# A SwiGLU feed-forward kernel on one core: three pairs of junk matmuls become two whole-array ones, and one early projection group also waits for x rows 768-1023

## The chip, the core and the metric

The kernel runs on one core of one Trainium2 chip. The core has a matmul engine (PE, with its weight loads shown apart as PEld), three elementwise engines (DVE, ACT, POOL), an engine that issues most transfers (SP) and 16 DMA engines that carry them. The metric is the device time of one launch in microseconds; the median of three runs before the change is 115.67 us (115.45 to 115.80). Lower is better.

## What is computed

```python
B, S, D, F = 1, 2048, 512, 1376        # all inputs bf16
def reference(x, w_gate, w_up, w_down):
    g = _silu(x @ w_gate)
    u = x @ w_up
    return (g * u) @ w_down
```

x is 2048 x 512, w_gate and w_up are 512 x 1376, w_down is 1376 x 512, the output is 2048 x 512.

## The kernel before, in words

Tokens are cut into four chunks c = 0 to 3 of 512; the 1376 hidden columns into ten F tiles ft = 0 to 9 of 128 and a rest of 96. x is needed with D on the partitions: the first 256 tokens are loaded plainly and transposed on PE with an identity, all later ones come in through transposing DMAs (L279). F tiles 0 to 3 of chunk 0 and 0 to 2 of chunk 1 are computed in the plain way ("classic"): a gate group and an up group of matmuls into one PSUM bank each, silu on ACT, and the product of the two on DVE into `h_sb`. Each group is eight matmuls (L424): four steps over D, each in two halves of 64 output rows that run side by side in the array.

All other F tiles are computed in 2 x 2 blocks (two F tiles by two chunks) with seven block products in place of eight (a Strassen-Winograd scheme). That needs sums of weight blocks (`ss_sb`, made by POOL, with casts by ACT) and sums of x blocks (`tt_sb`). For the first pair of chunks the four x sums T1 to T4 are made by DVE (L337, 128x1024 elements each) and the remaining operand is cast by ACT (L541); POOL's further weight sums stand behind T4. The products run on PE as L616 (fp32 sums) and L628 (plain bf16). The down projection follows (L726, L754, L864, L876).

Every piece of work is entered into a plan. PE's and SP's orders are the order of entry; ACT, DVE and POOL take, at each step of a simulated clock, whichever piece can start first, so the modelled landing times of loads (`land`) move pieces on these engines. From the finished order the plan derives semaphore waits; a wait that an earlier one on the same engine already implies is dropped. A PE instruction that needs several semaphores is preceded by a wait instruction of its own.

The loads that matter here, in SP's order: `xn` (tokens 0-255), `wg0` and `x0b` (gate columns 0-255, tokens 256-511), `wu0` (up columns 0-255), `wg2`, `wu2` (columns 256-511), `x1a` (tokens 512-767), `x1b` (tokens 768-1023), `wg4`, `wu4`, `wg8`, `wu8` and so on. Their semaphores are named below by number: s_dma14 xn, s_dma30 wg0, s_dma22 x0b, s_dma21 wu0, s_dma29 wg2, s_dma20 wu2, s_dma0 x1a, s_dma1 x1b, s_dma12 wg4, s_dma28 wu4, s_dma2 wg8, s_dma3 wu8.

While the first loads are under way PE runs matmuls on constant ones, into banks nobody reads (L350, L353 and, between the transposes and the first projection, L397). The program order of PE is then: chunk 0 gate tiles 0 and 1, up tiles 0 and 1, gate tiles 2 and 3, up tiles 2 and 3, then chunk 1.

## Time and profile before

| what | value |
|---|---|
| median of three runs | 115.67 us (115.45 to 115.80) |
| the profiled execution's own time | 115.52 us |
| its span, first to last instruction | 114.2 us |
| ACT busy, DVE busy, POOL busy | 64.0, 76.5, 62.2 us |
| bytes read from and written to HBM | 4.75 MB and 2.10 MB |

The profile shows one execution. Each engine has its instructions with start and duration; "idle before" is the time in which the engine had nothing running, with what ended it. The chain of waits is the path that ended last, followed back from the last instruction. For a DMA the profile gives the issue and the time from issue to landing, that is until the last part of its semaphore arrived. The difference between the span and the execution's own time, 1.3 us, lies outside the instructions and is taken as fixed.

### The profile page before, as it was taken

Reading aid. Unit: us, or ns where it says so; the run is one execution under the profiler, and the core shown is the slowest. Engines: PE = TensorE matmul, PEld = TensorE weight load, DVE = VectorE, ACT = ScalarE, POOL = GpSimd, SP = SyncE. Lnnn points to the kernel's source line nnn. Section 1 sums busy time; section 2 is a strip of 40 time slices with the busy share of each in tenths; the row PEclk is TensorE's granted clock in tenths of the full one; section 3 lists DMA queues with packets and bytes.
Section 4 is the critical chain, followed back from the end, with each engine's and each line's share of the span. In section 5 each row is a group of like instructions: output and inputs, shape, how many; then the busy total and the mean of one; then the engine's idle time right before and its main releaser. Section 6 shows DMA issues by size and latency. Waiting matters only on the chain.

```text
span 114.2 us, 1765 instructions
## 1 busy us (share of the span) xinstructions
PE 110.7 (97%) x646; PEld 68.0 (60%) x654; DVE 76.5 (67%) x113; ACT 64.0 (56%) x123; POOL 62.2 (54%) x61
## 2 busy tenths in 40 slices
PE   7999999999999999999999999999999999999993
PEld 2665555456674858576776858653344557866452
DVE  0113799883956858493948668499999957486423
ACT  5344765866679895867678786740567960000000
POOL 1493004999999999999998999845000000000000
PEclk9999999999999999999999999999999999999999
DMA  3999999994000000000000000000031002227976
GB/s 101 235 276 237 321 190 225 271 361 101 0 0 0 3 0 3 0 0 6 0 3 0 0 0 0 0 0 0 17 127 46 0 0 46 46 52 183 201 200 197
DMA packets 22808, 9.84 MB, mean 86 GB/s; under 512 B 12848, under 2 KB 22672, under 8 KB 22800
## 3 DMA queue, kind: packets, MB, share of 16 engines
q1 hardware_dynamic: 20656, 8.69, 31.5%
q10 hardware_dynamic: 2144, 1.05, 3.2%
q8 instruction: 5, 0.08, 0.3%
q14 instruction: 3, 0.02, 0.1%
HBM read 4.75 MB, written 2.10 MB: 60 GB/s over the span
## 4 chain that ended last, share of the span: by engine, by line
PE 96%; DVE 1%; issue 1%
PE psum L616 32%; PE psum L726 15%; PE psum L628 12%; PE psum L424 11%; PE psum L864 10%; PE psum L876 4%; PE psum L488 3%; PE psum L754 3%; PE psum L350 2%; PE psum L435 2%; PE psum L514 2%; DVE o_sb L326 1%; PE psum L397 0%; PE psum L380 0%; PE psum L373 0%
## 5 line engine op out<-in xcount | busy, mean ns | idle before, releaser
L616 PE MATMUL psum<-tt_sb,ss_sb 128*128 128x512 f32 x160 | 40.0, 403 | 0.0
L616 PEld LDWEIGHTS psum<-tt_sb,ss_sb 128*128 128x128 f32 x160 | 29.7, 188 | 7.9 <-DVE ts_sb L337 0.6
L337 DVE TENSOR_TENSOR ts_sb<-r_sb,psum 128x512 f32<-128x512 f32 x32 | 20.6, 681 | 14.9 <-ACT r_sb L325 14.9
L337 POOL TENSOR_TENSOR h_sb<-sg_sb,ts_sb 128x512 bf16<-128x512 f32 x16 | 20.9, 1309 | 2.8 <-ACT sg_sb L332 2.8
L332 ACT ACTIVATE sg_sb<-psum 128x512 f32<-128x512 f32 x24 | 14.3, 599 | 11.2 <-PE psum L616 6.0
L325 ACT ACTIVATE r_sb<-psum 128x512 f32<-128x512 f32 x32 | 17.3, 594 | 4.5 <-PE psum L616 4.5
L337 DVE TENSOR_TENSOR h_sb<-sg_sb,psum 128x512 bf16<-128x512 f32 x24 | 16.3, 681 | 4.2 <-PE psum L424 3.9
L337 POOL TENSOR_TENSOR ss_sb<-w_sb 128x512 fp32r<-128x512 bf16 (+1 forms) x12 | 11.8, 997 | 12.6 <-DVE tt_sb L337 9.0
L726 PE MATMUL psum<-wd_sb,h_sb 128*128 128x512 bf16 (+2 forms) x98 | 17.9, 336 | 0.2 <-issue 0.2
L628 PE MATMUL psum<-xT_sb,w_sb 128*128 128x512 bf16 x59 | 14.2, 380 | 0.4 <-issue 0.2
L726 PEld LDWEIGHTS psum<-wd_sb,h_sb 128*128 128x128 bf16 x100 | 8.3, 98 | 9.2 <-issue 1.0
L424 PE MATMUL psum<-xT_sb,w_sb 128*64 128x512 bf16 (+1 forms) x128 | 12.8, 359 | 0.0
L332 ACT ACTIVATE sg_sb<-ts_sb 128x512 f32<-128x512 f32 x16 | 10.1, 634 | 1.6 <-DVE ts_sb L337 1.6
L424 PEld LDWEIGHTS psum<-xT_sb,w_sb 128*64 128x64 bf16 x128 | 7.3, 114 | 5.4 <-DMA w_sb<-in_w_up_dram 0.3
L628 PEld LDWEIGHTS psum<-xT_sb,w_sb 128*128 128x128 bf16 x64 | 5.5, 98 | 8.0 <-issue 2.5
L326 DVE COPY psum<-psum 128x512 f32<-128x512 f32 x8 | 5.6, 699 | 1.2 <-PE psum L616 0.5
L337 POOL TENSOR_TENSOR ss_sb<-w_sb,ss_sb 128x512 fp32r<-128x512 bf16 (+1 forms) x6 | 6.0, 1007 | 0.3
L337 POOL TENSOR_TENSOR ss_sb<-ss_sb,w_sb 128x512 fp32r<-128x512 f32 (+1 forms) x6 | 6.0, 1000 | 0.0
L326 DVE CAST o_sb<-psum 128x512 bf16<-128x512 f32 (+2 forms) x6 | 3.0, 512 | 4.2 <-PE psum L726 3.1
L337 POOL TENSOR_TENSOR ss_sb<-wd_sb 128x640 fp32r<-128x640 bf16 x4 | 5.6, 1406 | 0.0
L864 PE MATMUL psum<-tt_sb,ss_sb 128*128 128x512 f32 x20 | 5.6, 417 | 0.0
L864 PE MATMUL psum<-th_sb,ss_sb 128*128 128x512 f32 x20 | 5.5, 411 | 0.0
(72 smaller groups left out, 121.4 us busy)
## 6 DMA issues: line engine op xcount, KB each, us to landing
wd_sb<-in_w_down_dram SPq DMA_DIRECT2D x1, 1280.0 KB, 8.5
w_sb<-in_w_gate_dram SPq DMA_DIRECT2D x4, 256.0 KB, 4.0
w_sb<-in_w_up_dram SPq DMA_DIRECT2D x4, 256.0 KB, 4.2
out_dram<-o_sb SPq DMA_DIRECT2D x7, 128.0 KB, 1.8
out_dram<-xT_sb ACTq DMA_DIRECT2D x4, 128.0 KB, 2.5
out_dram<-xT_sb ACTq DMA_DIRECT2D x2, 256.0 KB, 3.2
w_sb<-in_w_gate_dram SPq DMA_DIRECT2D x1, 352.0 KB, 5.2
w_sb<-in_w_up_dram SPq DMA_DIRECT2D x1, 320.0 KB, 5.6
```

What stands on the lines that cost most here:

```text
L325: return e.activation(out, src, ACT.Copy)
L326: return e.tensor_copy(out, src)
L332: "A", lambda e: e.activation(out, src, ACT.Silu), reads, writes, busy, A_LAG, prio
L337: engs, lambda e: e.tensor_tensor(out, a, b, alu), reads, writes, busy,
L424: ins = e.matmul(psum[h:h + HC, b, n0:n1], lhsT=w_sb[:, dk, m, ft * P + h:ft * P + h + HC], rhs=xT_sb[:, dk, c * SC + n0:c * SC + n1], sta ...
L488: ins = e.matmul(psum[m:m + HC, b, :], lhsT=w_sb[:, dk, 0, XC0 + m:XC0 + m + HC], rhs=xT_sb[:, dk, c * SC:(c + 1) * SC], start=(dk == 0), ...
L616: ins = e.matmul(bank(dst), lhsT=s[:, k, :], rhs=t[:, k, :], start=(start and k == 0), stop=(k == KH - 1), skip_group_check=True,)
L628: ins = e.matmul(bank(dst), lhsT=w_sb[:, k0 + k, m, f:f + P], rhs=xT_sb[:, k0 + k, c:c + SC], start=(start and k == 0), stop=(k == KH - 1) ...
L726: ins = e.matmul(psum[:, b, 0:c1 - c0], lhsT=hrows(F_ORDER[n], t, 0, P), rhs=wd_sb[:, F_ORDER[n], c0:c1], start=(start and n == n0), stop= ...
L754: ins = e.matmul(bank(b), lhsT=lhsT, rhs=rhs, start=(start and n == 0), stop=(n == 2 and (kind == "T" or not start)), tile_position=(r0, 0 ...
L864: ins = e.matmul(bank(dst), lhsT=self.ds[s][:, j, self.q, :], rhs=self.dt[t][:, j, :], start=(start and n == 0), stop=(n == NFF // 2 - 1), ...
L876: ins = e.matmul(bank(dst), lhsT=wd_sb[:, 2 * j + a, d * P:(d + 1) * P], rhs=h0_sb[:, 2 * j + a, 0:SC], start=(n == 0), stop=(n == NFF // ...
```

## The change

Three things. (1) The junk matmuls: the pair of 64-row matmuls at L353 becomes one matmul over the whole 128 x 128 array with 128 columns; the two pairs at L397 (512 and 128 columns) become one whole-array matmul with 512 columns. (2) The up group of F tile 3 of chunk 0 gets a further read, the key `x1b`: it waits for tokens 768-1023, which it does not use. (3) The modelled landing of a load becomes 0.4 us after its modelled transfer for all loads, where it was 0.3 us for early and 1.6 us for later ones.

```diff
-N_FILL = 1
-N_BETWEEN = (512, 128)
+N_BETWEEN = 512
@@ load
-            plan.add("S", emit, writes=writes, busy=busy, lag=1800, dma=(i, 16)).land = landed + (300 if landed < 10500 else 1600)
+            plan.add("S", emit, writes=writes, busy=busy, lag=1800, dma=(i, 16)).land = landed + 400
@@ warm
-            for i in range(N_FILL):
-                for h in range(2):
-                    ins = e.matmul(
-                        psum[:, NB - 2 + h, 0:P], lhsT=ones_w[h * HC:(h + 1) * HC, :],
-                        rhs=ones_m[h * HC:(h + 1) * HC, 0:P], start=True, stop=True, tile_position=(h * HC, 0),
-                    )
-            return ins
+            return e.matmul(psum[:, NB - 2, 0:P], lhsT=ones_w, rhs=ones_m[:, 0:P], start=True, stop=True)
@@ between
-            for n in N_BETWEEN:
-                for h in (0, HC):
-                    ins = e.matmul(
-                        psum[h:h + HC, NB - 1, 0:n], lhsT=ones_w[:, 0:HC], rhs=ones_m[:, 0:n],
-                        start=True, stop=True, tile_position=(0, h),
-                    )
-            return ins
+            return e.matmul(
+                psum[:, NB - 1, 0:N_BETWEEN], lhsT=ones_w, rhs=ones_m[:, 0:N_BETWEEN], start=True, stop=True
+            )
@@ gu_group
-            pe(emit, x_keys(c) + [f"w{'gu'[m]}{slab_of[ft]}"], [("b", b)], KD)
+            behind = ["x1b"] if (m, ft, c) == (1, 3, 0) else []
+            pe(emit, x_keys(c) + behind + [f"w{'gu'[m]}{slab_of[ft]}"], [("b", b)], KD)
```

The first place is PE's start, from the junk matmul behind the warm-up to the first projection. Before (the names are output<-operands; L373 and L380 are the transposes of x):

```order
L353 MATMUL psum<-const-bfloat16-1.0 128x128 x2
L373 MATMUL psum<-ident,xn_sb 128x64 [waits s_dma14,s_D]
L373 MATMUL psum<-ident,xn_sb 128x64 x11
L380 MATMUL psum<-ident,xn_sb 64x128 x4
L397 MATMUL psum<-const-bfloat16-1.0 64x512 x2
L397 MATMUL psum<-const-bfloat16-1.0 64x128 x2
L424 MATMUL psum<-xT_sb,w_sb 64x256 [waits s_dma30,s_D]
```

and with the change:

```order
L350 MATMUL psum<-const-bfloat16-1.0 128x128
L366 MATMUL psum<-ident,xn_sb 128x64 [waits s_dma14,s_D]
L366 MATMUL psum<-ident,xn_sb 128x64 x11
L373 MATMUL psum<-ident,xn_sb 64x128 x4
L388 MATMUL psum<-const-bfloat16-1.0 128x512
L413 MATMUL psum<-xT_sb,w_sb 64x256 [waits s_dma30,s_D]
```

Six junk matmuls became two, each with its weight load, so everything on PE from the first projection on stands eight instructions earlier in PE's program (the line numbers fall by 3 to 11).

The second place is on PE too: gate tiles 2 and 3, up tiles 2 and 3 of chunk 0, and the first gate group of chunk 1. Before:

```order
L424 MATMUL psum<-xT_sb,w_sb 64x512 [waits s_dma29]
L424 MATMUL psum<-xT_sb,w_sb 64x512 x15
L424 MATMUL psum<-xT_sb,w_sb 64x512 [waits s_dma20]
L424 MATMUL psum<-xT_sb,w_sb 64x512 x15
L424 MATMUL psum<-xT_sb,w_sb 64x512 [waits s_dma1,s_dma0,s_A]
L424 MATMUL psum<-xT_sb,w_sb 64x512 x7
```

and with the change:

```order
L413 MATMUL psum<-xT_sb,w_sb 64x512 [waits s_dma29]
L413 MATMUL psum<-xT_sb,w_sb 64x512 x15
L413 MATMUL psum<-xT_sb,w_sb 64x512 [waits s_dma20]
L413 MATMUL psum<-xT_sb,w_sb 64x512 x7
L413 MATMUL psum<-xT_sb,w_sb 64x512 [waits s_dma1]
L413 MATMUL psum<-xT_sb,w_sb 64x512 x7
L413 MATMUL psum<-xT_sb,w_sb 64x512 [waits s_dma0,s_A]
L413 MATMUL psum<-xT_sb,w_sb 64x512 x7
```

The wait for x1b (s_dma1) moved from chunk 1's first group up to the group ahead of it, the up group of tile 3; that of x1a (s_dma0) stayed.

The third place is ACT, from the cast of x to the silu of chunk 1's tile 2 (L541 casts: s_dma12 wg4, s_dma28 wu4, s_dma2 wg8, s_dma3 wu8). Before:

```order
L541 ACTIVATE tt_sb<-xT_sb 128x512 [waits s_dma1,s_dma0]
L541 ACTIVATE tt_sb<-xT_sb 128x512
L541 ACTIVATE ss_sb<-w_sb 128x256 [waits s_dma12]
L332 ACTIVATE sg_sb<-psum 128x512 [waits s_P]
L541 ACTIVATE ss_sb<-w_sb 128x256 [waits s_dma28]
L332 ACTIVATE sg_sb<-psum 128x512 [waits s_P]
L541 ACTIVATE ss_sb<-w_sb 128x256 [waits s_dma2]
L541 ACTIVATE ss_sb<-w_sb 128x256 [waits s_dma3]
L332 ACTIVATE sg_sb<-psum 128x512 [waits s_P]
```

and with the change:

```order
L531 ACTIVATE tt_sb<-xT_sb 128x512 [waits s_dma1,s_dma0]
L531 ACTIVATE tt_sb<-xT_sb 128x512
L531 ACTIVATE ss_sb<-w_sb 128x256 [waits s_dma12]
L531 ACTIVATE ss_sb<-w_sb 128x256 [waits s_dma28]
L331 ACTIVATE sg_sb<-psum 128x512 [waits s_P]
L531 ACTIVATE ss_sb<-w_sb 128x256 [waits s_dma2]
L331 ACTIVATE sg_sb<-psum 128x512 [waits s_P]
L531 ACTIVATE ss_sb<-w_sb 128x256 [waits s_dma3]
L331 ACTIVATE sg_sb<-psum 128x512 [waits s_P]
```

The casts of wu4 and of wg8 each went ahead of one silu. The work and its order on DVE, POOL and SP are as before; POOL's first sum behind the x sums no longer names wu4, whose arrival DVE's T4 now implies.

More of the change, by code (lines that the diff above doesn't have):

```diff
@@ L394, in between @@
         def between(e):
-            for n in N_BETWEEN:
-                for h in (0, HC):
-                    ins = e.matmul(
-                        psum[h:h + HC, NB - 1, 0:n], lhsT=ones_w[:, 0:HC], rhs=ones_m[:, 0:n],
-                        start=True, stop=True, tile_position=(0, h),
-                    )
-            return ins
-        pe(between, (), [("b", NB - 1)], sum(N_BETWEEN) / SC)
+            return e.matmul(
+                psum[:, NB - 1, 0:N_BETWEEN], lhsT=ones_w, rhs=ones_m[:, 0:N_BETWEEN], start=True, stop=True
+            )
+        pe(between, (), [("b", NB - 1)], 1)
         n_group = 0
```

## The prediction

> **What bounds the kernel now.** I read the page first, then the chain of waits in order of time, then the timeline of the first 24 us.

> ```profile
> span 114.2 us, 1765 instructions
> PE 96%; DVE 1%; issue 1%
> ```

> The chain is PE nearly throughout: what PE waits for, or does more of, goes to the end; the rest counts only through PE. The chain's pieces for the block products, twenty L616 matmuls each, show where PE is not at its own pace:

> ```profile
> 6.97 10.55 PE psum L424 x96
> ...
> 30.02 4.58 PE psum L616 x20
> ...
> 36.34 4.77 PE psum L616 x20
> ...
> 42.85 4.63 PE psum L616 x20
> ...
> 55.53 4.56 PE psum L616 x20
> ```

> The best piece takes 4.56 us; the one at 36.34 has 0.21 more, the one at 42.85 0.07 more. All that is left to win behind the start is some 0.3 us, if anything frees PE there. Now the start, where the change is made:

> ```profile
> 4.61 2.06 PEld L424 LDWEIGHTS psum<-xT_sb,w_sb 128*64 128x64 bf16 x32 [0.24 <-DVE xT_sb L326]
> ...
> 6.97 4.89 PEld L424 LDWEIGHTS psum<-xT_sb,w_sb 128*64 128x64 bf16 x48 [0.30 <-DMA w_sb<-in_w_up_dram]
> ...
> 12.09 1.15 ACT L541 ACTIVATE tt_sb<-xT_sb 128x512 fp32r<-128x512 bf16 x2 [0.83 <-DMA xT_sb<-in_x_dram]
> 12.10 4.93 PEld L424 LDWEIGHTS psum<-xT_sb,w_sb 128*64 128x64 bf16 x48 [0.24 <-issue]
> 12.12 1.23 DVE L337 TENSOR_TENSOR tt_sb<-xT_sb 128x1024 fp32r<-128x1024 bf16 x1 [2.43 <-DMA xT_sb<-in_x_dram]
> ...
> 17.33 1.22 DVE L337 TENSOR_TENSOR tt_sb<-xT_sb,tt_sb 128x1024 fp32r<-128x1024 bf16 x1
> ...
> 18.69 2.27 POOL L337 TENSOR_TENSOR ss_sb<-w_sb 128x512 fp32r<-128x512 bf16 x2 [9.01 <-DVE tt_sb L337]
> ```

> At 6.97 PE is released by wu0, so whatever happens before is hidden as long as it costs less than the 0.30 us waited. At 12.1 three engines start within 30 ns on x of chunk 1: DVE after 2.43 us of idleness, ACT after 0.83, and PE's loads, which stop for 0.24 us. The matmuls lose nothing (the chain has no gap in its 96): before, x1b arrives just in time. T4 (17.33) and POOL (18.69) hang on DVE's late start.

> When x1b landed is read from its issue, the second transposing DMA of chunk 1, and from the DMA traffic around 10 us:

> ```profile
> L279 SPq DMA_TRANSPOSE xT_sb<-in_x_dram x1: 1507/1507/1507, 7.0 to 7.0; - x1
> DMA to landing us min/median/max: 5.0/5.0/5.0
> ...
> DMA packets 43, 0.02 MB, mean 55 GB/s; under 512 B 0, under 2 KB 43, under 8 KB 43
> ...
> q8 instruction: 1, 0.02, 134.5%
> ```

> The first two rows are x1b's: issued at 7.0, complete at 12.0. The third is the traffic between 10.0 and 10.4 us: no packet under 512 B begins there. A row of a 256-column weight slab is 512 B, so what is smaller here is the transposed x: x1b's data had all been started by 10.0. The fourth is the window 9.85 to 9.90: one instruction packet of 0.02 MB begins in it, just as x1b ends. I read this as the cause of the two late microseconds: one of the 16 DMA engines had to carry the instruction block ahead of its share of x1b's completion.

> [...]

> What sets the moment of that block is seen by counting PE's matmuls and loads between the five instruction packets of this queue (windows that end where each begins; the x counts of PE and PEld):

> ```profile
> 0.00:9.86 9.86, 9.06 (x88) 5.11 (x90) 2.11 (x5) 4.02 (x9) 5.63 (x13) 1.00 0.90 215
> 9.86:26.78 16.92, 16.76 (x138) 8.87 (x136) 13.73 (x19) 11.97 (x23) 7.84 (x7) 1.00 1.08 263
> 26.78:53.49 26.71, 26.57 (x117) 18.41 (x118) 17.36 (x28) 20.72 (x42) 26.28 (x24) 1.00 0.01 3
> 53.49:81.23 27.74, 27.60 (x140) 17.62 (x140) 21.24 (x31) 17.18 (x34) 22.42 (x19) 1.00 0.00 1
> 81.23:101.86 20.63, 20.34 (x107) 11.97 (x107) 16.77 (x22) 10.11 (x19) 0.00 (x0) 1.00 0.17 45
> ```

> Between packets PE executes 274, 235, 280 and 214 instructions, 251 on average, over stretches of 17 to 28 us: the blocks follow the count of PE's instructions (with some lead), not the clock.

> **The change part by part.** *The junk.* Six matmuls with their loads become two. L397's two pairs are one piece of the chain:

> ```profile
> 4.39 0.53 PE psum L397 x4
> ```

> The 128-column pair goes: by columns (128 of 640) about 0.11 of the 0.53 us, at most all of it. The pair at L353 becomes one matmul of as many columns: 0. The first projection starts 0.11 sooner and then waits for wu0 at 6.97 as before: 0 on the path. Were that cover gone, it would be a gain of 0.11.

> *Eight instructions fewer.* The block boundary keeps its place in the count, so it meets the program eight instructions later. In the classic stretch 48 loads take 5.13 us (6.97 to 12.10), as many matmuls with them: 53 ns an instruction, 0.43 us for eight. The instruction packet begins at about 9.86 + 0.43 = 10.29 us, behind x1b's last packet (10.0) rather than with it. Bounds: 0 (the lead over execution takes up the shift; then all stays as it is) and 8 x 62 ns = 0.5 us from the row 9.86:26.78 (274 in 16.92 us). I take 0.43, from the stretch itself.

> *x1b's landing.* Between 10.0 (its last packet starts) and 12.0 (as now). Without the packet in its way I take 10.5 as an estimate, a quarter of the way, since the rest of a landing is only the completion.

> *The new wait.* The up group of tile 3 begins eight loads ahead of chunk 1, whose loads were ready to go 0.24 us before 12.10: 11.86 - 8 x 0.107 (5.13 us over 48 loads) = 11.0 us. With x1b at 10.5 the wait costs 0, with a margin of 0.5. If x1b comes at 12.0, the group starts at 12.1 and chunk 1 behind it, one group of 0.86 us later than before; the matmuls had a cushion over their loads of up to 0.24 us, now part of the loss or not: 0.62 to 0.86 us on the path, 0.75 taken. Queued behind this wait on PE is everything; tile 3's product on DVE would follow.

> *DVE, ACT, POOL.* T1 can start at about 10.55 in place of 12.12. The products between the sums need PE's up groups: tile 2's ends near 11.5, before T1 does (11.8). So the chain to T4 keeps its length (12.12 to 18.55, 6.43 us), T4 ends near 17.0 and POOL starts near 17.1, 1.6 us sooner. ACT casts wu4 ahead of the silu of chunk 1's tile 0; that silu came at 13.45 and may now come half a microsecond later, but its product stands behind T3 on DVE: 0.

> What an earlier POOL is worth stands at 34 us:

> ```profile
> 32.92 1.17 POOL L337 TENSOR_TENSOR ss_sb<-w_sb,ss_sb 128x512 fp32r<-128x512 bf16 x1
> ...
> 34.13 0.72 ACT L541 ACTIVATE ss_sb<-w_sb 128x256 fp32r<-128x256 bf16 x2 [0.60 <-POOL ss_sb L337]
> 34.76 1.06 ACT L325 ACTIVATE r_sb<-psum 128x512 f32<-128x512 f32 x2
> ...
> 35.37 1.28 DVE L337 TENSOR_TENSOR ts_sb<-r_sb,psum 128x512 f32<-128x512 f32 x2 [2.42 <-ACT r_sb L325]
> ...
> 36.11 0.30 PEld L616 LDWEIGHTS psum<-tt_sb,ss_sb 128*128 128x128 f32 x2 [0.27 <-DVE ts_sb L337]
> 36.70 0.99 PEld L616 LDWEIGHTS psum<-tt_sb,ss_sb 128*128 128x128 f32 x5 [0.30 <-DVE ts_sb L337]
> ```

> POOL's sum ends at 34.1; ACT waits 0.60 us for it with its cast, so PE's products are copied out late (34.76), DVE adds late (35.37) and PE's loads stop twice. With POOL ahead, the 0.60 goes, and with it the 0.21 us that the piece at 36.34 has too many. Bounds: 0 (POOL is held there by its products of `h_sb`, which wait for PE) and 0.28 (the piece at 42.85 too). I take 0.21.

> **The sum**, against the profiled execution (115.52 us): 0 + 0 + 0 - 0.21 = 115.31 us. The median of the runs is 0.15 higher; the same gain taken from it gives 115.46. Runs above the profiled one may owe it to x1b landing a little later still, which this change would remove too, so I lean to the former: 115.35 us, own range 114.95 to 115.6.

> **The rivals.** *x1b is still late (slower).* The instruction packet meets x1b as now, because the shift is lost in the lead, or another transfer holds one engine back. The wait then sits one group too early: 115.52 + 0.75 = 116.27 us. It decides from the point at which x1b lands after 11.0. For it: before, x1b misses by 2 us. Against it: the packet began within 0.15 us of x1b's end, and 0.43 is three times that.

> *The landing is early, but nothing reaches PE.* POOL's lead is used up before 34 us, or another wait takes the place of ACT's: 115.5 to 115.7 us. For it: POOL has `h_sb` products in between that need PE; against: only one stands ahead of the sum at 32.92.

> *The clock rises late (slower).* The junk keeps PE busy while it is slow: the first six 512-column matmuls take 2.72 us, 453 ns each, against 10.55 us for the 48 pairs later, 220 a pair.

> ```profile
> 0.77 2.72 PE psum L350 x6
> ```

> If less junk left PE at half pace until, say, 8.8 us, the gate groups of 256 columns would end near 8.0 in place of 6.9 and the next 0.8 us would do half its work: about 1.4 us late, 116.9. Against it: the junk goes where the projection follows at once, so PE is idle no longer than before. [...]

> **How the numbers follow.** Forecast 0.60; late x1b 0.18; nothing reaches PE 0.14; late clock 0.05; a larger gain than the bounds allow 0.03. A measurement of this kernel tells about 0.3% (0.35 us) from no change, so faster means below 115.32: the larger part of the forecast (0.40) and the larger gain (0.03), 0.43. Same: the rest of the forecast (0.20) and 0.13 of the third case, 0.33. Slower: late x1b, late clock and 0.01, 0.24. The range 114.9 to 116.3 takes in the first and third case and half of the late x1b (0.09), and leaves out some 0.18.

> **What will show it.** Right: the first instruction packet at 10.2 to 10.4; x1b at about 10.5, 3.5 us after its issue; DVE's T1 and ACT's cast near 10.6; POOL's sum at about 17.1; no ACT wait for POOL near 34; the piece at 36.34 at 4.6. Wrong: PE loads idle ahead of the up group of tile 3, released by the DMA of x, with DVE's T1 beside it at 12.1 (late x1b); or a pair pitch of double length behind 6.97 (clock).

## The result, and the profile after

The changed kernel takes 116.20 us (median of five executions, 116.11 to 116.35); the kernel before, in the same comparison, 115.45 us (115.34 to 115.80). The ratio is 1.0059, its 95% interval 1.0039 to 1.0079. The change makes the kernel slower, by 0.75 us between the medians. The forecast was 115.35 us; the time came out 0.07 us from the 116.27 us of the rival "x1b is still late".

The page of the changed kernel, its span and its chain by engine, and then four pieces of its chain in order of time (start, duration, what):

```profile
span 114.9 us, 1764 instructions
PE 87%; SPq 5%; DMA 5%; DVE 1%; issue 0%
...
6.97 5.23 DMA xT_sb<-in_x_dram
12.24 6.23 PE psum L413 x56
...
37.29 4.56 PE psum L606 x20
...
43.59 4.62 PE psum L606 x20
```

Before, PE held 96% of the chain, from the first projection on. Now the chain leaves PE at 12.24 us and goes back through a DMA of x, issued at 6.97 and 5.23 us under way: that is x1b, and what it holds up is the up group of tile 3. The timeline of the changed kernel shows the same place, and what hangs on it (start, duration, engine, line, operation, then in brackets the idle time ahead and what ended it):

```profile
7.27 0.36 PEld L413 LDWEIGHTS psum<-xT_sb,w_sb 128*64 128x64 bf16 x6
...
12.24 5.75 PEld L413 LDWEIGHTS psum<-xT_sb,w_sb 128*64 128x64 bf16 x56 [0.95 <-DMA xT_sb<-in_x_dram]
12.24 6.23 PE L413 MATMUL psum<-xT_sb,w_sb 128*64 128x512 bf16 x56 [0.47 <-DMA xT_sb<-in_x_dram]
12.29 1.15 ACT L531 ACTIVATE tt_sb<-xT_sb 128x512 fp32r<-128x512 bf16 x2 [0.74 <-DMA xT_sb<-in_x_dram]
12.32 1.23 DVE L336 TENSOR_TENSOR tt_sb<-xT_sb 128x1024 fp32r<-128x1024 bf16 x1 [2.34 <-DMA xT_sb<-in_x_dram]
...
17.53 1.22 DVE L336 TENSOR_TENSOR tt_sb<-xT_sb,tt_sb 128x1024 fp32r<-128x1024 bf16 x1
...
18.83 2.28 POOL L336 TENSOR_TENSOR ss_sb<-w_sb 128x512 fp32r<-128x512 bf16 x2 [8.54 <-DVE tt_sb L336]
```

PE, ACT and DVE again start together on x1b, at 12.2 to 12.3 us. But where PE's 0.24 us of idle loads cost nothing before, its loads now idle 0.95 us and its matmuls 0.47. Behind that PE stands 0.95 us later than before: the piece of block products that began at 36.34 begins at 37.29. Of these 0.95 us, 0.30 were lost ahead of the change's wait: in this execution the up groups start with wu0 at 7.27, not 6.97. The wait's part is the other 0.65.

Then 0.21 us come back: this piece took 4.77 us and now takes 4.56. PE runs 0.95 us later there and POOL only 0.14 (18.83 against 18.69), so ACT's cast behind POOL's sum, which had waited 0.60 us, now starts without idling:

```profile
34.36 0.73 ACT L531 ACTIVATE ss_sb<-w_sb 128x256 fp32r<-128x256 bf16 x2
```

The next such piece begins 0.30 + 0.65 - 0.21 = 0.74 us later (43.59 against 42.85); the two profiled executions are 116.29 - 115.52 = 0.77 us apart. The 0.30 is a matter of this execution: in run 1 below, with the same junk, the up groups start at 6.90.

Why x1b was late again is seen in the DMA traffic of the changed kernel, first from 10.15 to 10.18 us (counts of packets by size, then the instruction queue: packets, MB, share), then from 10.18 to 11.10, then from 11.10 to 11.13:

```profile
DMA packets 19, 0.02 MB, mean 633 GB/s; under 512 B 13, under 2 KB 18, under 8 KB 18
q8 instruction: 1, 0.02, 200.8%
...
DMA packets 132, 0.07 MB, mean 73 GB/s; under 512 B 0, under 2 KB 132, under 8 KB 132
...
DMA packets 9, 0.00 MB, mean 120 GB/s; under 512 B 2, under 2 KB 9, under 8 KB 9
```

In the 30 ns in which the last small packets (those of transposed x) begin, one instruction packet begins too. The share counts its whole time against 16 engines for 30 ns, so it took 2.008 x 16 x 0.03 = 0.96 us, from 10.16 to 11.12. From 10.18 to 11.10 no small packet begins; two do as the block ends. By their sizes in the trace these belong to x1b's completion: a transposing load here ends with 32 packets of 4 bytes (x1a's 32 begin at 9.21 to 9.25 in the changed kernel; run 3 has all 32 of x1b by 10.41), and the changed kernel has 30 by 10.17 and the last two at 11.11 and 11.12. The kernel before has 30 by 9.98 and the last two at 10.92 and 10.93, as its block (9.86 to 10.94) ends. So 2 of the 32, one engine's share if they are spread evenly over the 16 engines, came only as the block ended, 0.94 us behind the others in both kernels, as the prediction supposed; the trace doesn't name the engine. From the last of them x1b takes another 1.1 us to land in both kernels (12.0 and 12.20), against 0.5 in run 3; that difference isn't explained.

The block did move, from 9.86 to 10.16 us, but x1b's load moved with it, and they met again.

### The profile page after: what moved, and what is told of

The parts are those of the page before. It is cut to its first block, busy times and chain, and to the rows that moved or that the text cites. A ratio compares the mean times of both kernels' runs of the same rounds, so it can differ in the third digit from the quotient of the medians.

```text
span 114.9 us, 1764 instructions
## 1 busy us (share of the span) xinstructions
PE 111.4 (97%) x650; PEld 67.7 (59%) x650; DVE 76.6 (67%) x113; ACT 64.4 (56%) x123; POOL 62.2 (54%) x61
## 4 chain that ended last, share of the span: by engine, by line
PE 87%; SPq 5%; DMA 5%; DVE 1%; issue 0%
PE psum L606 32%; PE psum L716 15%; PE psum L618 12%; PE psum L854 10%; PE psum L413 5%; DMA xT_sb<-in_x_dram 5%; PE psum L866 4%; PE psum L478 3%; SPq L278 3%; PE psum L744 3%; SPq L266 2%; PE psum L424 2%; PE psum L504 2%; DVE o_sb L325 1%; SPq L283 0%
## 5 line engine op out<-in xcount | busy, mean ns | idle before, releaser
L336 DVE TENSOR_TENSOR ts_sb<-r_sb,psum 128x512 f32<-128x512 f32 x32 | 20.6, 682 | 14.5 <-ACT r_sb L324 14.4
L331 ACT ACTIVATE sg_sb<-psum 128x512 f32<-128x512 f32 x24 | 14.3, 601 | 11.7 <-PE psum L606 6.3
L336 POOL TENSOR_TENSOR ss_sb<-w_sb 128x512 fp32r<-128x512 bf16 (+1 forms) x12 | 11.8, 998 | 12.8 <-DVE tt_sb L336 8.5
L716 PE MATMUL psum<-wd_sb,h_sb 128*128 128x512 bf16 (+2 forms) x100 | 18.4, 337 | 0.0
L618 PE MATMUL psum<-xT_sb,w_sb 128*128 128x512 bf16 x64 | 15.4, 381 | 0.0
L325 DVE COPY psum<-psum 128x512 f32<-128x512 f32 x8 | 5.6, 699 | 1.2 <-PE psum L606 0.5
L325 DVE CAST o_sb<-psum 128x512 bf16<-128x512 f32 (+2 forms) x6 | 3.0, 512 | 4.2 <-PE psum L716 3.1
```

Source lines behind the costliest of these rows:

```text
L325: return e.tensor_copy(out, src)
L331: "A", lambda e: e.activation(out, src, ACT.Silu), reads, writes, busy, A_LAG, prio
L336: engs, lambda e: e.tensor_tensor(out, a, b, alu), reads, writes, busy,
L618: ins = e.matmul(bank(dst), lhsT=w_sb[:, k0 + k, m, f:f + P], rhs=xT_sb[:, k0 + k, c:c + SC], start=(start and k == 0), stop=(k == KH - 1) ...
L716: ins = e.matmul(psum[:, b, 0:c1 - c0], lhsT=hrows(F_ORDER[n], t, 0, P), rhs=wd_sb[:, F_ORDER[n], c0:c1], start=(start and n == n0), stop= ...
```

## The experiments

Five theories. **A**: the wait alone costs the time, since x1b is late. **B**: the junk or the new landing model (the order on ACT and DVE) costs it. **C**: the instruction block is asked for by PE's count of instructions and begins only where a load ends on its DMA engine, so that a shift of eight instructions keeps it at the end of x1b (a supposition: the traces give the block's start, not what it waits for). **D**: the block is bound to a time or a place in the program. **E**, formed later: whole-array junk lets PE reach its full pace earlier. A sixth, **H**, came out of a run that contradicted A.

The table gives for each run when the instruction block begins (the window of DMA traffic in which its packet starts), when DVE's T1 starts (0.12 us after x1b has landed in the kernel before, at 12.0, and in the changed one, at 12.20) and the ratio to the kernel before on the same chip.

| run | edit | block, us | T1, us | ratio (95% interval) |
|---|---|---|---|---|
| before | | 9.86 | 12.12 | |
| changed | the change | 10.16 | 12.32 | 1.0059 (1.0039 to 1.0079) |
| 1 | changed, no wait | 9.97 | 12.27 | 1.0004 (0.9982 to 1.0025) |
| 2 | before, with the wait | 9.91 | 12.18 | 1.0041 (1.0018 to 1.0063) |
| 3 | 24 PE instructions fewer, no wait | 13.51 | 11.07 | 0.9980 (0.9961 to 0.9999) |
| 4 | 28 more, no wait | 9.22 | 12.25 | 0.9983 (0.9965 to 1.0002) |
| 5 | 48 fewer, no wait | 13.69 | 10.71 | 1.0007 (0.9989 to 1.0025) |
| 6 | 48 fewer, with the wait | 13.09 | 10.56 | 1.0011 (0.9992 to 1.0030) |
| 7 | 24 fewer, with the wait | 14.09 | 10.99 | 1.0009 (0.9982 to 1.0037) |
| 8 | 16 fewer, no wait | 10.61 | 11.43 | 0.9989 (0.9969 to 1.0009) |
| 9 | before, the wait on tile 2 | 14.35 | 11.14 | 0.9993 (0.9970 to 1.0017) |
| 10 | 56 fewer, changed junk, no wait | 13.67 | 10.39 | 1.0031 (1.0016 to 1.0047) |
| 11 | 24 fewer, changed junk, no wait | 11.21 | 11.11 | 1.0006 (0.9985 to 1.0027) |
| 12 | before, a wait for x1a on tile 2 | 13.77 | 10.85 | 0.9993 (0.9972 to 1.0014) |
| 13 | changed, with that wait for x1a too | 13.10 | 10.95 | 0.9993 (0.9975 to 1.0011) |
| 14 | changed, its wait moved to tile 2 | 13.79 | 10.67 | 1.0009 (0.9987 to 1.0031) |
| 15 | before, the wait on gate tile 3 | 14.89 | 11.27 | 1.0068 (1.0045 to 1.0091) |

### Which part of the change costs it (runs 1 and 2)

Run 1 is the changed kernel without its wait:

```diff
-            behind = ["x1b"] if (m, ft, c) == (1, 3, 0) else []
-            pe(emit, x_keys(c) + behind + [f"w{'gu'[m]}{slab_of[ft]}"], [("b", b)], KD)
+            pe(emit, x_keys(c) + [f"w{'gu'[m]}{slab_of[ft]}"], [("b", b)], KD)
```

> The changed kernel without the new wait: the junk matmuls and the landing model stay changed. Theory A (the wait alone loses, since x of tokens 768-1023 is still complete only near 12.1 us): 115.3 to 115.6 us, as before the change, with PE's loads stopping near 12.1 us for 0.3 us or less. Theory B (the junk matmuls or ACT's new order lose, by a slower start of PE): 116.0 to 116.3 us.

Run 2 is the kernel before with the same two lines the other way round.

> The kernel before with the new wait alone. Theory A: 116.1 to 116.4 us, as the changed kernel, with PE's loads idle for 0.9 us or so ahead of the up group of tile 3. Theory B: 115.3 to 115.6 us.

Run 1 is as fast as before. Its timeline, with a piece of its chain behind:

```profile
12.25 2.33 PEld L413 LDWEIGHTS psum<-xT_sb,w_sb 128*64 128x64 bf16 x24 [0.46 <-issue]
12.27 1.23 DVE L336 TENSOR_TENSOR tt_sb<-xT_sb 128x1024 fp32r<-128x1024 bf16 x1 [2.65 <-DMA xT_sb<-in_x_dram]
...
36.49 4.73 PE psum L605 x20
```

Run 2:

```profile
12.10 2.30 PEld L424 LDWEIGHTS psum<-xT_sb,w_sb 128*64 128x64 bf16 x24 [0.86 <-DMA xT_sb<-in_x_dram]
12.10 2.56 PE L424 MATMUL psum<-xT_sb,w_sb 128*64 128x512 bf16 x22 [0.38 <-DMA xT_sb<-in_x_dram]
12.18 1.23 DVE L337 TENSOR_TENSOR tt_sb<-xT_sb 128x1024 fp32r<-128x1024 bf16 x1 [2.25 <-DMA xT_sb<-in_x_dram]
...
37.15 4.56 PE psum L617 x20
```

The wait alone gives 0.41% (0.47 us), the rest of the change 0.04%: A, not B. Run 2 also shows the give-back: the piece near 37 us is down to 4.56, where run 1 without the wait keeps 4.73.

### What moves the block (runs 3 to 8)

These change the number of PE's instructions ahead of the block, and runs 6 and 7 add the change's wait to it. Run 3 is the changed kernel without its wait and with the transposes of x as eight whole-array matmuls; run 4 the kernel before with two of its six warm-up matmuls replaced by sixteen small ones; runs 5 and 8 the kernel before with the six full groups of chunk 0 (run 8: up tiles 0 and 1 alone) as four whole-array matmuls each instead of eight.

Run 3 (against the changed kernel without its wait):

```diff
-                    if dk < KD - 1:
-                        for h in range(2):
...
-                    else:
-                        for m in (0, HC):
...
+                    ins = e.transpose(tview(dk)[:, i, :], xn_sb[:, i, dk * P:(dk + 1) * P], ident[:, :])
```

> No new wait; the changed junk, and the transposes of the first 256 tokens as 8 whole-array matmuls in place of 16 halves: 24 PE instructions fewer ahead of the first projection than in the kernel before. Theory C (the instruction block is asked for at a place in the count of PE's instructions): it is asked for 1.3 us of program later, begins at 10.6 to 11.3 us, and x of tokens 768-1023 completes at 10.5 to 10.8 us, 3.5 us after its issue; DVE's first x sum starts near 10.8; the time gains up to 0.25 us: 115.1 to 115.5, if the slower transposes (some 0.35 us) stay hidden behind the load of w_up. Theory D (the block is bound to the time or to the place in the program, not to the count): it still begins as the x packets end, and x completes near 12.1.

Run 4:

```diff
-N_WARM = 6
+N_WARM = 4
...
+            for i in range(16):
+                e.matmul(psum[0:HC, NB - 1, 0:HC], lhsT=ones_w[:, 0:HC], rhs=ones_m[:, 0:HC], start=True, stop=True)
```

> The kernel before with two of the six 512-column junk matmuls replaced by sixteen of 64 x 64 and 64 columns: 28 PE instructions more ahead of the first projection, no new wait. Theory C: the instruction block is asked for 1.5 us of program sooner, begins at 8.2 to 9.3 us; x of tokens 768-1023 then completes at 11.0 to 11.6 us, since its DMA engine is still a microsecond behind, but its completion no longer stands behind the block itself. Time 115.2 to 115.6. Theory D: the block begins near 9.9 to 10.2 and x completes near 12.1 as before.

Run 5, and run 6 with the change's wait:

```diff
+            whole = whole or (c == 0)
```

> The kernel before, no new wait, the old junk; the six full groups of chunk 0 (up tiles 0 and 1, gate and up tiles 2 and 3) as four whole-array matmuls each in place of eight halves: the same columns streamed, 48 PE instructions fewer ahead of chunk 1. Theory C (count of instructions, and a start only between two loads): the block begins with or after the load behind x of tokens 768-1023, that is at 11 us or later; x completes at 10.3 to 10.8 us, DVE's first x sum starts by 10.9, PE has no wait near 12.1 and loses nothing near 36 us. Time 0.2 to 0.4 us below the kernel before, ratio 0.996 to 0.999. Theory D (bound to the time or the program's place): x completes near 12.1, ratio 0.999 to 1.002.

> The same with the new wait ahead of up tile 3. If the wait costs only because x is late (theory A with C): as the run without it, 0.996 to 0.999, no idle loads ahead of up tile 3. If the wait itself costs (a semaphore in PE's queue, whatever its time): 0.2 us or more above it, 1.000 or more.

Run 7, run 3 with the change's wait:

> The run with 24 PE instructions fewer (whole-array transposes, changed junk), with the new wait added. Theory A with C: x is complete near 10.9 us as there, the wait ends before PE reaches it at 11.6, ratio 0.996 to 1.000. If the wait itself costs: 1.002 to 1.006, as in the run with the wait alone.

Run 8:

```diff
+            whole = whole or ((m, ft, c) in ((1, 0, 0), (1, 1, 0)))
```

> The kernel before with only up tiles 0 and 1 of chunk 0 as whole-array matmuls: 16 PE instructions fewer. This looks for the edge. Theory C: the block is asked for some 0.9 us later than in the kernel before; if it was asked for in the second half of the transfer of x of tokens 768-1023 there (after 9.4 us), it now begins after that x, x completes at 10.3 to 10.8, ratio 0.996 to 0.999; if in the first half, it still begins as x ends, near 9.9 to 10.2, x completes near 12.1, ratio 0.999 to 1.002.

T1 in run 3, in run 4 and in run 5:

```profile
11.07 1.23 DVE L336 TENSOR_TENSOR tt_sb<-xT_sb 128x1024 fp32r<-128x1024 bf16 x1 [0.84 <-DMA xT_sb<-in_x_dram]
```
```profile
12.25 1.22 DVE L337 TENSOR_TENSOR tt_sb<-xT_sb 128x1024 fp32r<-128x1024 bf16 x1 [2.10 <-DMA xT_sb<-in_x_dram]
```
```profile
10.71 1.23 DVE L337 TENSOR_TENSOR tt_sb<-xT_sb 128x1024 fp32r<-128x1024 bf16 x1 [0.55 <-DMA xT_sb<-in_x_dram]
```

With 24 or 48 instructions fewer the block comes at 13 to 14 us and x1b is early, with 16 fewer it comes at 10.61, as x1b's last packets begin (10.6 to 10.74), but holds none of them up; with 8 fewer, none or 28 more it comes at 9.2 to 10.2 and x1b is late. So the block does follow PE's program, as predicted, and eight instructions are too few. Run 4 missed what was expected of it: the block met the end of x1a, which landed at 4.8 + 6.3 = 11.1 us in place of 9.6, and x1b landed at 12.1, not at 11.0 to 11.6. Where x1b is early the wait is free: run 6 costs 0.04% more than run 5, against 0.41% in run 2. Run 7 is 0.29% above run 3, which its wide interval can't tell from zero or from 0.41%; its profile shows no idle PE at the wait. But an early x1b gains nothing that these intervals can tell from zero (0.996 to 0.999 was expected of runs 5 and 6); only run 3 lies just below 1.

### A dose that gave no effect (run 9)

If x1b lands at 12.1 whatever PE does, the same wait one group earlier must cost a group more.

```diff
+            behind = ["x1b"] if (m, ft, c) == (1, 2, 0) else []
+            pe(emit, x_keys(c) + behind + [f"w{'gu'[m]}{slab_of[ft]}"], [("b", b)], KD)
```

> The kernel before, with the wait for x 768-1023 put on the up group of tile 2 of tokens 0-511 instead of tile 3: one group of 0.86 us earlier. Theory A (the loss is PE idle from the waiting group until x1b lands near 12.1): the stall grows by a whole group, so chunk 1's groups start at about 13.8 in place of 12.1, and the time is 115.77 + 0.75 + 0.86 - 0.25 = about 117.1 us (ratio about 1.012). If instead the loss comes from how the wait is carried (one semaphore more to test) or from another order on the other engines: 116.2 us as with the wait on tile 3 (ratio 1.004).

It cost nothing. The chain of run 9, its timeline, and the traffic around 14.35 us:

```profile
7.56 10.69 PE psum L424 x96
```
```profile
11.12 3.41 PEld L424 LDWEIGHTS psum<-xT_sb,w_sb 128*64 128x64 bf16 x34 [0.40 <-issue]
11.14 1.23 DVE L337 TENSOR_TENSOR tt_sb<-xT_sb 128x1024 fp32r<-128x1024 bf16 x1 [0.86 <-DMA xT_sb<-in_x_dram]
```
```profile
q8 instruction: 1, 0.02, 163.1%
```

The 96 matmuls take 10.69 us in place of 10.55: 0.14 us for the wait. x1b was not late, because the block came not at 9.9 but at 14.35 us, with not one PE instruction fewer ahead of it. Theory A as it stood falls: x1b's lateness is not given, it hangs on where the wait stands. Hence **H**, the author's reading: PE's sequencer runs ahead of its matmuls and asks for the block at one instruction, between the first loads of the up groups of tiles 2 and 3 (10.23 and 11.10 us in the kernel before, where the block begins at 9.86); a wait ahead of that instruction holds the request back until the load has landed; the change's wait stands behind it. The traces show when the block begins; the request itself is in none of them.

### The request held by another wait (runs 12 to 15)

Run 12, against the kernel before:

```diff
+            behind = ["x1a"] if (m, ft, c) == (1, 2, 0) else []
+            pe(emit, x_keys(c) + behind + [f"w{'gu'[m]}{slab_of[ft]}"], [("b", b)], KD)
```

> The kernel before, with a wait for x 512-767 (x1a, landed at about 9.5 us, before that group starts at 10.4) on the up group of tile 2 of tokens 0-511; no wait for x 768-1023 is added. Theory H (PE's sequencer, held at this wait, asks for the instruction block later): the block no longer begins at 9.9 us but behind 10.5, most likely behind wg4 or wu4 (11 to 14.3 us); x 768-1023 lands at 10.4 to 11.0 with DVE's first sum beside it; PE does not wait. Time 115.76 - 0.2 = about 115.55 us (0.998). Against it (the block's start follows the executed instructions or the clock): block at 9.9 us, x 768-1023 at 12.0, 115.76 us (1.000).

Run 13, against the changed kernel:

```diff
-            behind = ["x1b"] if (m, ft, c) == (1, 3, 0) else []
+            behind = {(1, 2, 0): ["x1a"], (1, 3, 0): ["x1b"]}.get((m, ft, c), [])
```

> The changed kernel, its wait for x 768-1023 left on tile 3, with a wait for x 512-767 added on the up group of tile 2. Theory H: the block comes later than 10.5 us, x 768-1023 lands at 10.4 to 11.0, the wait on tile 3 then costs nothing (no idle PE ahead of chunk 1 at 12), chunk 1's groups start at about 12.2 in place of 13.1: 116.2 - 0.6 = about 115.6 us (ratio to before 0.998). Against it: as the changed kernel, 116.2 to 116.3 us (1.005).

Run 14, against the changed kernel:

```diff
-            behind = ["x1b"] if (m, ft, c) == (1, 3, 0) else []
+            behind = ["x1b"] if (m, ft, c) == (1, 2, 0) else []
```

> The changed kernel with its wait moved from the up group of tile 3 to that of tile 2. Theory H: as the wait alone on tile 2, the block comes behind x 768-1023 (11 us or later), x 768-1023 lands at 10.4 to 11.0 and PE waits 0 to 0.3 us for it: about 115.6 us (0.998 to 1.000). Theory A alone (x 768-1023 lands near 12.1 whatever PE does): PE idle from 10.4 until 12.1, 116.2 + 0.86 = about 117.0 us (1.011).

Run 15, as run 9 but with `(0, 3, 0)`, the gate group of tile 3:

> The kernel before, with the wait for x 768-1023 on the gate group of tile 3 of tokens 0-511, one group ahead of the up group of tile 2. Theory H: block behind x 768-1023, which lands at 10.4 to 11.0; the group was ready at about 9.6, so PE now idles 0.8 to 1.4 us, little of it won back: 115.76 + 0.9 = about 116.7 us (1.008), with a gap of that size ahead of this group. Theory A alone (x 768-1023 near 12.1): idle 2.5 us, 118 us or more (1.02).

Run 12: the two transposing DMAs of chunk 1 (issues and time to landing), T1, and the traffic of 9.0 to 10.5 us (no instruction packet in it) and of 13.7 to 13.8:

```profile
L279 SPq DMA_TRANSPOSE xT_sb<-in_x_dram x2: 1722/1942/2161, 4.8 to 7.0; - x2
...
DMA to landing us min/median/max: 3.8/4.4/4.9
```
```profile
10.85 1.22 DVE L337 TENSOR_TENSOR tt_sb<-xT_sb 128x1024 fp32r<-128x1024 bf16 x1 [0.96 <-DMA xT_sb<-in_x_dram]
```
```profile
DMA packets 1262, 0.32 MB, mean 212 GB/s; under 512 B 1219, under 2 KB 1262, under 8 KB 1262
```
```profile
DMA packets 44, 0.04 MB, mean 439 GB/s; under 512 B 0, under 2 KB 43, under 8 KB 43
q8 instruction: 1, 0.02, 73.2%
```

x1a landed at 4.8 + 4.9 = 9.7 us, x1b at 7.0 + 3.8, about 10.8, where it took 5.0 before. A wait for x1a, a load that had landed before PE's turn at 10.4, moved the block from 9.9 to 13.77 us, and T1 from 12.12 to 10.85. It takes no instruction away (the wait instruction that it adds would, by run 4, move the block the other way: 9.22 us with 28 instructions more, against 9.86) and costs PE no time, so neither the count of executed instructions nor the clock explains it. What is shown is that the place of the wait moves the block; that the sequencer's request is what is held back, H, is the reading that fits. Run 13 puts the same wait into the changed kernel, whose wait for x1b stays on tile 3 (timeline, then a piece of the chain):

```profile
8.71 5.99 PE L413 MATMUL psum<-xT_sb,w_sb 128*64 128x512 bf16 x54
10.95 1.23 DVE L336 TENSOR_TENSOR tt_sb<-xT_sb 128x1024 fp32r<-128x1024 bf16 x1 [0.84 <-DMA xT_sb<-in_x_dram]
...
17.45 2.27 POOL L336 TENSOR_TENSOR ss_sb<-w_sb 128x512 fp32r<-128x512 bf16 x2 [7.26 <-DVE tt_sb L336]
...
33.82 0.73 ACT L531 ACTIVATE ss_sb<-w_sb 128x256 fp32r<-128x256 bf16 x2
```
```profile
36.75 4.56 PE psum L606 x20
```

PE runs from 8.71 to 14.7 without a stop, T1 and POOL are 1.2 us earlier than before, ACT waits for nobody at 33.82, the piece at 36.75 is at 4.56, and the loss is gone: 0.9993 (0.9975 to 1.0011) against 1.0059 (1.0039 to 1.0079). Run 14 (0.43 us of idle loads, no idle matmuls of note) is level with before as well:

```profile
10.65 3.84 PEld L413 LDWEIGHTS psum<-xT_sb,w_sb 128*64 128x64 bf16 x38 [0.43 <-issue]
10.67 1.23 DVE L336 TENSOR_TENSOR tt_sb<-xT_sb 128x1024 fp32r<-128x1024 bf16 x1 [0.89 <-DMA xT_sb<-in_x_dram]
```

In run 15 x1b is early too, but the group that waits for it could have begun at 9.9:

```profile
11.18 3.38 PEld L424 LDWEIGHTS psum<-xT_sb,w_sb 128*64 128x64 bf16 x34 [1.81 <-DMA xT_sb<-in_x_dram]
11.19 3.64 PE L424 MATMUL psum<-xT_sb,w_sb 128*64 128x512 bf16 x32 [1.33 <-DMA xT_sb<-in_x_dram]
```

1.33 us of idle matmuls, 0.68% (0.79 us) in the time. Both sides of H hold: with the instruction counts of the kernel before or the changed one, all five kernels with an added wait at the head of up tile 2 or earlier (runs 9 and 12 to 15) have the block at 13.1 us or later, and both with it at the head of up tile 3 alone (run 2 and the change) at 9.9 to 10.2. In those five x1b is early (T1 at 10.67 to 11.27), and an added wait for x1b costs PE what is left between the group's turn and about 11 us: 0.14 us in run 9, 1.33 us in run 15. The wait for x1a costs PE nothing (runs 12 and 13).

### Theory E, and the junk (runs 10 and 11)

Runs 10 and 11 are 5 and 8 with the changed junk.

> The changed kernel without its wait, and with the six full groups of tokens 0-511 as four whole-array matmuls each (56 PE instructions fewer than before). Theory C (the instruction block is begun only where a load ends on its DMA engine): the block comes behind wg4 or wu4 (13 to 14.5 us), x1b lands within 0.3 us of its first part, near 10.6, and DVE's first sum of chunk 1 starts with it. Theory E (the whole-array junk lets the pitch of the 256-column pairs fall from 0.213 to 0.109 us before 5.1 us, where the paired junk left it at 0.213 until 5.4 to 6.6): the up groups start with wu0, within 0.05 us of its landing. With both the time is 115.77 - 0.2 - 0.2 = about 115.35 us (ratio 0.996); if the earlier pitch is chance, 115.8 us as the same kernel with the paired junk gave (ratio 1.0007).

> The changed kernel without its wait, and with only the up groups of tiles 0 and 1 of tokens 0-511 as whole-array matmuls (24 PE instructions fewer than before, as many as in the run with the whole transposes). Theory C: the block is asked for 24 instructions (1.3 us) later than before, so behind x1b's load: x1b lands near 10.6 to 11.0. Theory E: pitch 0.109 us before 5.1 us, up groups with wu0. Time about 115.4 us (ratio 0.997); if the earlier pitch is chance, 115.75 us (ratio 0.999, as with the paired junk and 16 fewer).

In most runs with the paired junk the first gate groups ran at half pace, 0.21 us from pair to pair of 256 columns, until 5.4 to 6.6 us (until 5.35 in the kernel before, then 0.11); in most with the whole-array junk they ran at 0.11 us from the start (from 5.03 in the changed kernel). But run 11, with the new junk, has the slow pace, and run 10 the fast one (loads of these groups, 32 each):

```profile
4.89 2.39 PEld L413 LDWEIGHTS psum<-xT_sb,w_sb 128*64 128x64 bf16 x32 [0.44 <-DVE xT_sb L325]
```
```profile
4.41 1.68 PEld L413 LDWEIGHTS psum<-xT_sb,w_sb 128*64 128x64 bf16 x32 [0.23 <-DVE xT_sb L325]
```

Runs 9 and 12, with the old junk, were fast too (16 such loads in 0.82 us each, as in the changed kernel). As a rule E falls; whether the junk shifts the odds is open. Neither run gained: run 11 is level, run 10 is slower by 0.31%. Why run 10 loses with x1b early, and with no stop of PE's matmuls over 0.16 us behind 7.02, stays open.

## Why the prediction was wrong

By its own steps:

- **The junk, 0.** Right: junk and landing model together give 1.0004 (0.9982 to 1.0025), run 1.
- **Eight instructions fewer.** This is the step that failed: "The instruction packet begins at about 9.86 + 0.43 = 10.29 us, behind x1b's last packet (10.0) rather than with it." That the block follows PE's program was right (runs 3 to 8). Its time, 10.16, came within 0.13, by luck. What failed is "behind x1b's last packet". Counted from the start of the up groups, the block came 9.86 - 6.97 = 2.89 us after it before and 10.16 - 7.27 = 2.89 now: no shift in this execution, and x1b's own packets ended at 10.18 instead of 10.0. Run 1, with the same eight fewer, has 9.97 - 6.90 = 3.07, again with x1b's last packets. What happened is the lower bound that the prediction gave this step, 0. Whether the lead over execution took up the shift, as it put it there, or the block, asked for later, could still begin only with the end of the same load, these runs don't separate. By H the request stood between the heads of up tiles 2 and 3 in both kernels (runs 2 and 12; the changed kernel and run 13). A margin of 0.29 us against one time of one execution was taken for the distance to the edge; eight instructions fewer do not reach it; with sixteen fewer the block still began with x1b's last packets but held none of them (run 8).
- **x1b's landing, 10.5.** It failed with the step above: x1b landed at 12.2. As a size it was about right: without the block x1b is in at 10.3 to 11.1, 0.1 ahead of T1 (runs 3, 5 to 7, 9 to 15).
- **The new wait, 0, and the price if x1b is late.** The bounds 0.62 to 0.86 hold the 0.65 of the profile, 0.75 taken; the net 0.41 to 0.59% (0.47 to 0.68 us) is smaller, since 0.21 us come back near 36 us. The prediction didn't count this give-back in its rival; its 116.27 came close to the profiled 116.29 by luck, because the start was 0.30 us later as well.
- **T1, POOL, ACT at 34 us, the gain of 0.21.** As a chain this was right: run 13, in which x1b is early, shows each of its links. The gain itself is not resolved: 0.9993 allows a gain of up to 0.29 us and a loss of up to 0.13. From one execution to the next the start of the up groups alone varies as much (6.97 before, 7.27, 7.56 in run 9).
- **The rivals.** "x1b is still late" is what happened, by its mechanism: the block meets x1b as before. "The clock rises late" is not the cause: in the changed kernel the up groups follow wu0 at 7.27, and their pairs stand 0.21 to 0.22 us apart from 7.51 on, as in the kernel before from 7.21 on.

## What to carry to other kernels

Before a wait is moved ahead to a load that is "about in time", look at what ends that load, and whether an instruction packet begins just then. Here one did, at 9.86 us before and 10.16 with the change, as x1b's last packets began, and x1b landed at 12.0 and 12.20 us, against about 10.8 in run 12 with the packet at 13.77. A wait that cost nothing (run 12's, at the head of up tile 2, for a load that had landed at 9.7) moved the packet out of the way; the change's wait for the late load itself, one group further on, paid for it with 0.47 us of idle matmuls. And a forecast that rests on 0.3 us between two transfers of one execution needs the test whether both move together.

## What was not expected of the hardware

- One instruction block of 16384 bytes, 1.08 us under way in the kernel before and 0.96 in the changed one, in the way of a load of 256 rows, goes with a landing of the whole load over a microsecond later: T1 starts at 12.1 to 12.3 us with the block at 9.2 to 10.2, at 10.4 to 11.3 with the block at 11 us or later. PE itself shows no such loss in the kernel before: behind 6.97 its matmuls stop for no longer than 0.16 us.
- The block, once held, came 3 to 4 us later, not the 1 us or less by which the wait can have held it (x1a had landed by 9.7 in run 12, the block would have begun at 9.9 and began at 13.77). What it waited for in that time no run here shows.
- The time from the last copy to the end of the span, in which the last stores land, varies by 0.9 us between the profiled executions (1.68 us in the kernel before, 2.56 in run 14). The copies of run 10 and of the kernel before that end each chain:

```profile
111.31 0.87 DVE o_sb L325 x3
```
```profile
111.63 0.88 DVE o_sb L326 x3
```

  The first ends at 112.18 and the span at 114.4 us, the second at 112.51 and 114.2. So 0.3 us won ahead of the last copy were lost behind it. This, too, hides gains of the size that was forecast.
